# A decode layer on one core: the query projection in rows of 512, wo's last rows as 2 KB rows reordered on TensorE, W_down's last rows loaded at the end of the queue

## Chip, cores, metric

One core of a Trainium2 chip. The metric is the device time of one execution in microseconds, the median of repeated runs. The profile's span (first to last recorded instruction) is about 1.26 us shorter than the time.

## The reference

```python
# x [2,1,512]; k_cache, v_cache [2,32,8192,128]; wq [512,4096]; wo [4096,512]
# W_gate, W_up [512,1376]; W_down [1376,512]; all bf16
h  = x + A(layernorm(x))          # A: q = x@wq; softmax(q.K/sqrt(128)) @ V per head; then @ wo
h2 = h + B(layernorm(h))          # B: (relu(x@W_gate) * (x@W_up)) @ W_down
```

Two batch rows, 32 heads, 8192 cached keys: 268 MB of K and V are read once, and each is used with a single query. The weights are 12.6 MB more.

## The kernel before

One tile is K or V of two heads of one batch row: 128 partitions of 32 KB, 4 MB. Four slots hold two K and two V tiles. SyncE issues all large loads, in order, on one queue spread over 16 DMA engines.

The start of the queue, and the query projection (cut):

```python
nc.sync.dma_start(slot[3][:], A_wq...).then_inc(sem_wq, 16)
load(0, A_k_cache, 0)
load(1, A_v_cache, 0)
nc.sync.dma_start(wo_last[:].rearrange("p (h n) -> p h n", n=D),          # 256 runs of 1 KB
    A_wo[128 * DR:].rearrange("(h d) n -> d h n", d=128)).then_inc(sem_wl, 16)
nc.sync.dma_start(wd_last[:], B_W_down[F - FR:]).then_inc(sem_wd[3], 16)  # 96 runs of 1 KB
load(2, A_k_cache, 1)
# ... layernorm of x, transposed ...
for h in range(H):
    for c in range(DC):                                                   # 128 matmuls, 2 columns each
        i = nc.tensor.matmul(Wp[:, h*B:(h+1)*B], lhsT=wq[:, c, h*Dh:(h+1)*Dh], rhs=lT[:, c*B:(c+1)*B], ...)
# ... qT -> q_all: eight rounds of a DVE copy, four matmuls, one ScalarE copy ...
```

The loop over pairs of tiles (cut). VectorE multiplies 96 of the 128 key columns of a K tile with q and adds; TensorE does the other 32 through transposes, then all of P·V. The K slot is refilled after VectorE's multiply and TensorE's last transpose:

```python
run_d(k_mult(q)); last_d(); nc.vector.sem_inc(d2s, 1)     # VectorE has read the K tile
...
sp.wait((d2s, p + 1), tokp("kf", p)); load(s, A_k_cache, p + 2)
```

The end of the kernel (cut): W_up, W_gate and W_down go into the slot of the last-but-one K tile. W_up and W_gate become 44 small matmuls each; W_down is 11 blocks f of 4 matmuls, in the order of four DMAs:

```python
pe.wait((sem_wd[3], 16), t_hd)
order = [(10, 3)] + [(f, k) for k, (r0, n) in enumerate(WD_BLOCKS) for f in range(r0, r0 + n)]
for n, (f, k) in enumerate(order):
    pe.wait((sem_wd[k], 16))
    for m in range(4):
        i = nc.tensor.matmul(Op[0][32*m:32*m+B, 0:128], lhsT=hd[0:kp, f*B:(f+1)*B], rhs=..., ...)
```

A block in the text below is 256 instructions of a program unless it is called a block of W_down.

The softmax here doesn't subtract the row's maximum and nothing guards it: scores larger than these inputs give would overflow.

## Time and profile before

| | before |
|---|---|
| time, median of 3 | 661.2 us (661.18 to 661.27) |
| bytes moved, mean rate | 281.17 MB, 426 GB/s |
| spacing of 4 MB tiles, landing to landing, 50 to 625 us | 9.71 us |
| VectorE's first multiply in the loop | 26.05 us |
| last landing / last W_down matmul starts / end of span | 656.36 / 657.02 / 659.7 us |

The profile page of the kernel before. In the rows of forty slices a DMA digit of 9 is a share of 90% or more. The line that begins with q8 is the queue that brings instructions: packets, MB, share of the 16 engines' time. The last line is the summary of the chain that ended last.

```profile
span 659.7 us, 7791 instructions
...
DMA  9999999999999999999999999999999999999997
...
DMA packets 10781, 281.17 MB, mean 426 GB/s; under 512 B 1202, under 2 KB 1556, under 8 KB 1940
...
q8 instruction: 5, 0.08, 0.0%
...
DMA 80%; DVE 18%; issue 1%; PE 1%; SPq 0%; DVEq 0%
```

The queue is never empty: this is a kernel bound by its bytes. The 18% of VectorE in the chain are the multiplies that free a K slot; each is followed in the chain by a load of 32 us, of which only 9.7 us are its own transfer, the rest is queueing behind earlier tiles. So a quicker VectorE would only lengthen that queueing.

The timeline of the kernel before at the start of its loop (start, duration, engine, line, operation; in brackets the idle time before it and what ended it):

```profile
24.43 1.09 ACT L300 ACTIVATE q_all<-O 128x512 bf16<-128x512 f32 x2 [0.28 <-PE O L295]
26.05 6.56 DVE L514 TENSOR_TENSOR prod<-slot,q_c 128x12288 bf16<-128x12288 bf16 x1 [2.02 <-POOL q_c L511]
32.70 0.33 SPq L169 DMA_DIRECT2D slot<-in_A_k_cache_dram  x1
```

The load that this first multiply sets free is issued at 32.70 us and lands at 73.39 us, for X, V1 and the rest of K1 are ahead of it. Some 30 us of it are slack.

The chain of waits of the kernel before, its last pieces in order of time (start, length, what):

```profile
627.07 26.18 DMA slot<-in_B_W_gate_dram
...
653.30 1.73 PE O L730 x44
...
655.13 0.18 DVE hd L763
...
655.46 1.01 PE O L782 x29
656.47 0.28 issue
656.74 0.61 PE O L782 x14
```

W_gate lands, 44 matmuls, the gated product hd, and W_down's 44 matmuls, among which there is a hole. The timeline of the same matmuls:

```profile
655.46 0.28 PE L782 MATMUL O<-wd_last,hd 96*2 96x128 bf16 x4 [0.31 <-DVE ve L773]
655.52 0.95 PE L782 MATMUL O<-slot,hd 128*2 128x128 bf16 x25
656.74 0.59 PE L782 MATMUL O<-slot,hd 128*2 128x128 bf16 x15 [0.28 <-issue]
```

Matmul starts are exact in the records, ends are modelled. From the start of the 29th matmul (656.16) to that of the 30th (656.74) TensorE starts nothing for 0.59 us. The releaser is "issue", that is, none that the profile shows, and the 30th carries no wait; the wait for the last W_down DMA stands six weight loads later.

### The profile page before, as it was taken

How to read it: one execution, taken by the hardware profiler on the slowest of the kernel's cores; microseconds unless marked ns; L12 is line 12 of the kernel's file. 1: busy time of each engine (PE TensorE's matmuls, PEld its weight loads, DVE VectorE, ACT ScalarE, POOL GpSimd, SP SyncE). 2: the span in 40 equal slices, each digit the busy share in tenths (PEclk: the TensorE clock that was granted, in tenths of full speed). 3: DMA queues.
4: the chain of work that ended last, by engine and by line, in shares of the span. 5: the costliest groups of instructions: out<-in, count | busy, mean ns of one | idle time of the engine just before them, and what ended most of it. 6: DMA issues, size and time to landing. Idle time of an engine off the chain costs nothing.

```text
span 659.7 us, 7791 instructions
## 1 busy us (share of the span) xinstructions
PE 323.9 (49%) x3173; PEld 194.0 (29%) x3173; DVE 471.7 (71%) x285; ACT 211.9 (32%) x428; POOL 72.1 (11%) x121
## 2 busy tenths in 40 slices
PE   2653344435456443635545363554446554353577
PEld 2431322223233222323323242322324322132344
DVE  1775576788767678776768867676876767787991
ACT  0622332243342233333223243323324322333240
POOL 2002002020200202020020201102020110202000
PEclk9999995567755567675555757555575555657657
DMA  9999999999999999999999999999999999999997
GB/s 382 431 416 427 439 421 443 429 429 437 421 442 423 439 431 427 437 423 439 431 431 435 423 441 421 441 435 423 437 424 437 431 431 435 425 439 423 439 417 291
DMA packets 10781, 281.17 MB, mean 426 GB/s; under 512 B 1202, under 2 KB 1556, under 8 KB 1940
## 3 DMA queue, kind: packets, MB, share of 16 engines
q1 hardware_dynamic: 10760, 281.06, 99.3%
q8 instruction: 5, 0.08, 0.0%
q14 instruction: 4, 0.03, 0.0%
q10 hardware_dynamic: 12, 0.00, 0.0%
HBM read 281.05 MB, written 0.00 MB: 426 GB/s over the span
## 4 chain that ended last, share of the span: by engine, by line
DMA 80%; DVE 18%; issue 1%; PE 1%; SPq 0%; DVEq 0%
DMA slot<-in_A_k_cache_dram 76%; DVE prod L514 16%; DMA slot<-in_B_W_gate_dram 4%; DVE prod L523 2%; PE O L730 0%; PE O L782 0%; DVE scores L528 0%; SPq L169 0%; SPq L175 0%; DVEq L561 0%; SPq L178 0%; DVEq L565 0%; SPq L172 0%; DVE kT L789 0%; DVE hd L763 0%
## 5 line engine op out<-in xcount | busy, mean ns | idle before, releaser
L514 DVE TENSOR_TENSOR prod<-slot,q_c 128x12288 bf16<-128x12288 bf16 x32 | 209.9, 6558 | 145.8 <-DMA slot<-in_A_k_cache_dram 142.7
L379 PE MATMUL O<-slot,e 128*16 128x512 bf16 x1024 | 118.4, 617 | 220.0 <-ACT e L469 146.3
L523 DVE TENSOR_TENSOR prod<-prod 128x6144 bf16<-128x6144 bf16 (+3 forms) x128 | 212.3, 1658 | 7.8
L540 ACT ACTIVATE kT<-T 128x1024 bf16<-128x1024 bf16 x128 | 126.2, 1022 | 145.9 <-PE T L355 143.3
L355 PE MATMUL T<-ident_f,slot 128*128 128x128 f32 x512 | 111.5, 373 | 29.1 <-DVEq L561 29.0
L379 PEld LDWEIGHTS O<-slot,e 128*16 128x16 bf16 x1024 | 26.3, 113 | 286.3 <-ACT e L469 173.0
L469 ACT ACTIVATE e<-scores 64x96 bf16<-64x96 f32 x64 | 19.4, 304 | 239.7 <-DVEq L575 238.9
L355 PEld LDWEIGHTS T<-ident_f,slot 128*128 128x128 f32 x512 | 80.9, 191 | 44.3 <-DVEq L561 44.3
L511 POOL COPY q_c<-q_all 128x136 bf16<-128x136 bf16 x32 | 57.2, 1789 | 197.8 <-DVEq L565 167.8
L338 PE MATMUL S<-q_c,kT 128*128 128x4 bf16 x1024 | 47.5, 168 | 39.6 <-ACT kT L540 38.9
L338 PEld LDWEIGHTS S<-q_c,kT 128*128 128x128 bf16 x1024 | 39.4, 104 | 67.1 <-ACT kT L540 65.9
L391 PE MATMUL Ob<-sel,os_sb 128*128 128x4 f32 x136 | 30.1, 345 | 24.0 <-ACT os_sb L543 24.0
L391 PEld LDWEIGHTS Ob<-sel,os_sb 128*128 128x128 f32 x136 | 28.7, 312 | 25.9 <-ACT os_sb L543 25.9
L494 POOL MEMSET O_l<- 128x40 bf16 (+1 forms) x13 | 1.8, 136 | 303.8 <-DVEq L572 303.8
L528 DVE TENSOR_REDUCE scores<-prod 128x96 f32<-128x768 bf16 x32 | 30.5, 953 | 2.8
L540 ACT ACT_TABLE_LOAD x15 | 19.2, 1283 | 0.3
L469 ACT ACTIVATE e<-S 64x32 bf16<-64x32 f32 x64 | 13.0, 202 | 15.1 <-PE S L338 14.7
L543 ACT ACTIVATE os_sb<-O 128x512 f32<-128x512 f32 x17 | 10.2, 597 | 11.8 <-PE O L379 11.4
L469 ACT ACTIVATION_READ_ACCUMULATOR e<-S 64x1 f32 x64 | 12.8, 201 | 0.7
L469 ACT ACTIVATION_READ_ACCUMULATOR e<-scores 64x1 f32 x64 | 11.8, 184 | 0.0
L400 PEld LDWEIGHTS Ob<-zs,ones_f 128*128 128x128 f32 x30 | 7.3, 305 | 12.8 <-issue 12.8
L300 ACT ACTIVATE q_all<-O 128x512 bf16<-128x512 f32 x8 | 4.3, 595 | 17.7 <-PE O L295 17.7
(94 smaller groups left out, 91.7 us busy)
## 6 DMA issues: line engine op xcount, KB each, us to landing
slot<-in_A_k_cache_dram SPq DMA_DIRECT2D x32, 4096.0 KB, 32.1
slot<-in_A_v_cache_dram SPq DMA_DIRECT2D x31, 4096.0 KB, 30.3
slot<-in_A_wq_dram SPq DMA_DIRECT2D x1, 4096.0 KB, 12.2
X<-in_A_wo_dram SPq DMA_DIRECT2D x1, 3840.0 KB, 46.6
slot<-in_A_v_cache_dram SPq DMA_DIRECT2D x1, 3072.0 KB, 23.1
slot<-in_B_W_up_dram SPq DMA_DIRECT2D x1, 1376.0 KB, 23.2
slot<-in_B_W_gate_dram SPq DMA_DIRECT2D x1, 1376.0 KB, 26.2
slot<-in_A_v_cache_dram SPq DMA_DIRECT2D x1, 1024.0 KB, 25.2
```

The source lines that it names most:

```text
L338: i = nc.tensor.matmul(Sp[p % 2][:, 2 * jj:2 * jj + 4], lhsT=kv_[:, k, r, :], rhs=q_c[p % 2][:, 4 * r:4 * r + 4], start=(r == 0), stop=(r ...
L355: i = nc.tensor.transpose(Tp[g % 2][:, k * 128:(k + 1) * 128], k_t[:, j:j + 2, :].rearrange("p j d -> p (j d)").bitcast(F32), ident_f[:])
L379: i = nc.tensor.matmul(Op[0][c:c + 16, :], lhsT=e_t[q][:, j // VJ, :], rhs=v_t[:, j:j + VJ, :].rearrange("p j d -> p (j d)"), start=(q == ...
L391: i = nc.tensor.matmul(Ob[:, 0:4], lhsT=os_sb[:, jj * Dh:(jj + 1) * Dh], rhs=sel[:, 4 * jj:4 * jj + 4], start=(jj == 0), stop=(jj == VJ - 1))
L400: return nc.tensor.matmul(bank[:, ZC:ZC + 8], lhsT=ones_f[:], rhs=zs[:], start=True, stop=True)
L469: i = nc.scalar.activation(out=e_t[q][h, j0 // VJ:j1 // VJ, 8 * q:8 * q + 8].rearrange("p g (j a) -> p g j a", a=2)[:, :, :, a], in_=src(h ...
L511: nc.gpsimd.tensor_copy(out=q_c[p % 2][:], in_=q_all[:, p]).then_inc(g2d, 1)
L514: return nc.vector.tensor_tensor(out=prod[:, 0:JC, :], in0=tile((2 * p) % 4)[:, 0:JC, :], in1=q_c[p % 2][:, 8:QW].unsqueeze(1).broadcast_t ...
L523: run(nc.vector.tensor_tensor(out=prod[:, 0:JC, 0:w], in0=prod[:, 0:JC, 0:w], in1=prod[:, 0:JC, w:2 * w], op=ALU.add))
L528: return nc.vector.tensor_reduce(out=scores[p % PG][:, 0:JC], in_=prod[:, 0:JC, 0:8], axis=AX.X, op=ALU.add)
L540: to_pe(nc.scalar.activation(out=kT[gg % 2][:], in_=Tp[gg % 2][:].bitcast(BF16), func=ACT.Copy))
L543: to_pe(nc.scalar.activation(out=os_sb[:], in_=Op[0][:], func=ACT.Copy))
```

## The change

The intent: fewer, wider matmuls in the projection, fewer small packets, and a start of the queue without the 352 rows of 1 KB.

```diff
                 nc.sync.dma_start(slot[3][:], A_wq.rearrange("(p c) n -> p (c n)", c=DC)).then_inc(sem_wq, 16)
+                nc.sync.dma_start(
+                    wo_rows, A_wo[128 * DR:].rearrange("(p r) n -> p (r n)", r=2)).then_inc(sem_wl, 16)
                 load(0, A_k_cache, 0)
                 load(1, A_v_cache, 0)
-                nc.sync.dma_start(
-                    wo_last[:].rearrange("p (h n) -> p h n", n=D),
-                    A_wo[128 * DR:].rearrange("(h d) n -> d h n", d=128)).then_inc(sem_wl, 16)
-                nc.sync.dma_start(wd_last[:], B_W_down[F - FR:]).then_inc(sem_wd[3], 16)
                 load(2, A_k_cache, 1)
 # ... cut: the constants pick and place, made on GpSimd ...
-                for h in range(H):
+                for i in range(2):
                     for c in range(DC):
-                        i = nc.tensor.matmul(
-                            Wp[:, h * B:(h + 1) * B], lhsT=wq[:, c, h * Dh:(h + 1) * Dh],
-                            rhs=lT[:, c * B:(c + 1) * B], start=(c == 0), stop=(c == DC - 1))
+                        for t in range(4):
+                            n = (2 * t + i) * 512
+                            mm = nc.tensor.matmul(
+                                Op[i][32 * t:32 * t + B, :], lhsT=lT[:, c * B:(c + 1) * B], rhs=wq[:, c, n:n + 512],
+                                start=(c == 0), stop=(c == DC - 1))
 # ... cut: two evictions, 8 transposes; then in place of eight DVE copies and 32 matmuls:
+                for m in range(8):
+                    for a in range(2):
+                        mm = nc.tensor.matmul(
+                            Op[m % 2][64 * a:64 * a + 64, :], lhsT=pick[:, m, :],
+                            rhs=q_row.rearrange("p (m a d) -> p m a d", a=2, d=Dh)[:, :, a, :], start=True, stop=True)
 # ... one ScalarE copy each, as before ...
+                pe.wait((sem_wl, 16))
+                for h in range(2):
+                    for r in range(2):
+                        mm = nc.tensor.matmul(
+                            Tp[h][:], lhsT=place[:, h, r, :], rhs=wo_rows[:, r * D:(r + 1) * D], start=(r == 0), stop=(r == 1))
+                    t = pe.run(mm)
+                    act.wait(t)
+                    t_wl = act.run(nc.scalar.activation(out=wo_last[:, h * D:(h + 1) * D], in_=Tp[h][:], func=ACT.Copy))
 # ... at the end of the queue, behind the other W_down blocks:
+                        nc.sync.dma_start(wd_last[:], B_W_down[F - FR:]).then_inc(sem_wd[3], 16)
-                pe.wait((sem_wd[3], 16), t_hd)
-                order = [(10, 3)] + [(f, k) for k, (r0, n) in enumerate(WD_BLOCKS) for f in range(r0, r0 + n)]
+                pe.wait(t_hd)
+                order = [(f, k) for k, (r0, n) in enumerate(WD_BLOCKS) for f in range(r0, r0 + n)] + [(10, 3)]
```

## The prediction

> **What bounds the kernel now.** The profile page counts 281.17 MB moved at a mean 426 GB/s, and the row of DMA shares is 9 in every slice but the last. The chain of waits that ended last is 80% DMA and 18% the DVE multiply that frees a K slot. That DVE share is no bottleneck: the queue is never empty. From landing to landing of the 4 MB tiles the trace shows 9.71 us all the way from 50 to 625 us. So time is bytes, plus the start, plus what follows the last landings (the timeline: W_gate 653.3, last W_down block 656.4, last W_down matmul 657.3, output copies 657.8, end 659.7).
>
> **The three parts, costed.**
>
> 1. Query projection. Before: 128 matmuls with 2 columns (3.6 us), then eight DVE copies, 32 matmuls and eight ScalarE copies; the loop's first multiply starts at 26.05 us. After: 32 matmuls of 512 columns, two evictions, 8 transposes, 16 matmuls, the same eight ScalarE copies of about 0.6 us, two more for wo. I estimate a loop start 1 to 3 us earlier. Worth nothing: the K slot freed by that multiply (32.7 us) is refilled by a load behind 10 MB in the queue, landing at 73.4 us; there is some 30 us of slack.
>
> 2. wo rows. Its 256 packets of 1 KB took 46 ns each, W_down's 128 packets of 2 KB took 85 ns: over 16 engines 0.74 against 0.68 us. The median landings show wo_last costing 0.82 us. Gain about 0.1 us, directly on the DMA stream. The Trainium skill, "DMA: Bandwidth & Descriptors", section "Why small descriptors are slow", names a fixed overhead per packet; the packet times agree.
>
> 3. wd_last (96 KB, 0.38 us by landing times) moves from the early queue to its end. Same bytes; up, gate and the other W_down blocks land about 0.5 us earlier, the last landing about 0.2 us earlier, and 4 matmuls instead of 8 follow it.
>
> 4. A side effect. 100 fewer matmuls: some 200 PE instructions less before the loop. The Trainium skill, "Runtime: NRT & Kernel Launch", section "Instruction fetch mechanics", says blocks of 256 instructions are fetched by DMA. This trace shows five 16 KB instruction packets, the last at 654.15 us, and a PE pause inside the last W_down matmuls, 656.16 to 656.74, at which no semaphore wait stands: I read it as a block arriving late. After, I count one fetch fewer, and the last boundary falls near the start of the W_down matmuls, where its block should be there in time. Each fetch also leaves one DMA engine about 1.4 us late for good (a tile's sixteen landing marks: one straggler after the first, two after the second), and the slowest engine sets every landing. They fell on different engines, so one fewer should not change the maximum (1.8 us).
>
> **Sum.** 0.1 to 0.2 us from the stream, 0.3 to 0.6 us from the end of W_down: about 0.7 us. I predict 660.5 us, range 659.7 to 661.3. Faster by over 2%: 1%; within 2%: 98%; slower by over 2%: 1%.
>
> **What would show it right.** Four instruction packets of 16 KB; tile spacing still 9.71 us; the loop starting earlier without K2 landing earlier than by 0.2 us; no pause inside the last W_down matmuls; last matmul near 656.6 us; tail from last matmul to end still 2.3 us.
>
> **What would make it wrong.** Two fetches on one DMA engine would make it about 3 us late and cost about 1.4 us. A pause at the moved block boundary would return the gain. If the small rows at the queue's end land with more delay than amid large ones, W_down ends no earlier.

## The result

The changed kernel takes 660.47 us (median of 6 runs, 660.21 to 660.55); the kernel before beside it 661.21 us (6 runs, 660.97 to 661.27). The ratio is 0.9989, with a 95% interval of 0.9976 to 1.0001. Ratios are the mean time of one kernel's runs over that of the other's of the same rounds, so not quite the ratio of the medians. The interval lies far inside 2% and contains 1, so by itself it does not show which kernel is faster. In this measurement and in two controls on two different chips (below) the medians differ by -0.74, -0.60 and -0.78 us, and in the first and the last of them every run of the changed kernel was below every run of the one before.

The page of the changed kernel:

```profile
span 659.2 us, 7582 instructions
...
DMA packets 10653, 281.17 MB, mean 427 GB/s; under 512 B 1202, under 2 KB 1300, under 8 KB 1812
...
q8 instruction: 5, 0.08, 0.1%
...
DMA 76%; DVE 19%; PE 4%; issue 1%; ACT 1%; SPq 0%; DVEq 0%
```

128 packets fewer (256 of 1 KB became 128 of 2 KB), the same bytes, and 209 executed instructions fewer. Tiles still land 9.71 to 9.72 us apart. The 4% of PE in the chain are new; where they come from is seen below. The timeline at the start of the loop:

```profile
23.67 1.08 ACT L318 ACTIVATE q_all<-O 128x512 bf16<-128x512 f32 x2 [0.25 <-PE O L312]
25.12 0.60 ACT L329 ACTIVATE wo_last<-T 128x512 bf16<-128x512 f32 x1 [0.36 <-PE T L325]
25.93 0.60 ACT L329 ACTIVATE wo_last<-T 128x512 bf16<-128x512 f32 x1 [0.21 <-PE T L325]
26.85 6.56 DVE L540 TENSOR_TENSOR prod<-slot,q_c 128x12288 bf16<-128x12288 bf16 x1 [5.73 <-ACT wo_last L329]
```

The loop starts 0.8 us later, not earlier: ScalarE's eight copies take their 0.6 us each as before, the two copies of wo come behind them, and VectorE waits for those. The chain at the end of the changed kernel:

```profile
651.30 1.71 PE S L756 x44
653.01 0.34 PE T L767 x14
653.36 1.66 PE O L756 x44
...
655.13 0.19 DVE hd L789
...
655.36 1.37 PE O L808 x23
```

W_gate is no longer in this chain: it landed at 652.5 us and TensorE came to it at 653.3. And the W_down matmuls of its timeline:

```profile
655.36 1.23 PE L808 MATMUL O<-slot,hd 128*2 128x128 bf16 x40 [0.22 <-DVE hd L789]
656.38 0.32 PE L808 MATMUL O<-wd_last,hd 96*2 96x128 bf16 x4
```

All 44 run in one go; the last starts at 656.39 us instead of 657.02. That is 0.63 us sooner; the spans differ by 0.55 us, for what follows that matmul took 0.08 us longer. The sum: hd starts at the same 655.13 us in both; the first W_down matmul follows 0.10 us sooner (0.23 instead of 0.33 us behind hd); the hole of 0.59 us is gone; the 44 matmuls themselves took 0.05 us more. (The profiled pair is one execution of each kernel; below, other executions lose their time elsewhere.)

### The profile page after: what moved, and what is told of

It reads as the page before. It is cut to its first block, busy times and chain, and to the rows that moved or that the text cites. A ratio compares the mean times of both kernels' runs of the same rounds, so it can differ in the third digit from the quotient of the medians.

```text
span 659.2 us, 7582 instructions
## 1 busy us (share of the span) xinstructions
PE 324.3 (49%) x3073; PEld 188.6 (29%) x3073; DVE 469.2 (71%) x280; ACT 213.6 (32%) x431; POOL 73.5 (11%) x125
## 4 chain that ended last, share of the span: by engine, by line
DMA 76%; DVE 19%; PE 4%; issue 1%; ACT 1%; SPq 0%; DVEq 0%
DMA slot<-in_A_k_cache_dram 76%; DVE prod L540 16%; DVE prod L549 2%; PE O L405 1%; PE O L463 1%; PE T L381 0%; ACT kT L566 0%; PE W L469 0%; DVE scores L554 0%; PE S L756 0%; PE O L756 0%; PE O L808 0%; PE Ob L417 0%; SPq L172 0%; PE S L364 0%
## 5 line engine op out<-in xcount | busy, mean ns | idle before, releaser
L381 PE MATMUL T<-ident_f,slot 128*128 128x128 f32 x512 | 108.6, 365 | 29.1 <-DVEq L587 29.1
L381 PEld LDWEIGHTS T<-ident_f,slot 128*128 128x128 f32 x512 | 79.0, 188 | 44.2 <-DVEq L587 43.3
L525 POOL COPY rsel<-rows 128x30 bf16<-128x30 bf16 x28 | 5.9, 209 | 33.3 <-DVEq L598 32.5
```

The costliest lines, as they stand in the source:

```text
L381: i = nc.tensor.transpose(Tp[g % 2][:, k * 128:(k + 1) * 128], k_t[:, j:j + 2, :].rearrange("p j d -> p (j d)").bitcast(F32), ident_f[:])
```

## The experiments

The question is which part brings this, and why. The theory of the prediction: the hole is TensorE waiting for a block of instructions that its DMA has not yet brought, because the queue is full of weights; 206 instructions fewer before the loop move that block's boundary. The rival: what counts is the landing of the last weights, so the part that loads at the end brings most, and the parts add up.

All twelve runs gave correct results. Each was timed in 5 rounds, four kernels to a chip. Medians in us:

| kernel | time | before, same chip | span (median of its runs) | span before, same chip |
|---|---|---|---|---|
| wd_alone | 660.83 | 661.04 | 659.6 | 659.8 |
| q_alone | 660.67 | 661.04 | 659.4 | 659.8 |
| wo_alone | 661.05 | 661.04 | 659.8 | 659.8 |
| after_pad | 660.62 | 661.04 | 659.4 | 659.8 |
| after_same | 660.52 | 661.12 | 659.3 | 659.9 |
| before_pad | 661.84 | 661.12 | 659.7 | 659.9 |
| late_loop | 660.31 | 661.12 | 659.1 | 659.9 |
| hr_late | 660.40 | 661.12 | 659.2 | 659.9 |
| after_ctl | 660.42 | 661.20 | 659.2 | 660.0 |
| not_wd | 661.13 | 661.20 | 659.8 | 660.0 |
| not_wo | 660.30 | 661.20 | 659.1 | 660.0 |
| hr_late_b | 660.32 | 661.20 | 659.1 | 660.0 |

The intervals of the ratios are all about 0.13% to each side (0.9 us), so a single difference of 0.2 us in this table is not resolved. What decides are the traces: in each the last W_down matmul can be followed back to what it waited for.

| profiled run | hd starts | first W_down matmul | hole (us) | last landing | last W_down matmul | what was last |
|---|---|---|---|---|---|---|
| before | 655.13 | 655.46 | 0.59 | 656.36 | 657.02 | hole, behind the chain to hd |
| after | 655.13 | 655.36 | none | 656.06 | 656.39 | TensorE's chain to hd |
| wd_alone | 655.15 | 655.39 | 0.47 | 656.09 | 656.85 | hole, behind the chain to hd |
| q_alone | 655.29 | 655.62 | none | 656.53 | 656.65 | landing |
| wo_alone | 655.66 | 655.99 | 0.18 | 656.39 | 657.04 | chain to hd, hole |
| after_pad | 655.41 | 655.65 | 0.07 | 656.40 | 656.68 | chain to hd, hole |
| after_same | 655.24 | 655.48 | none | 656.08 | 656.51 | chain to hd |
| before_pad | 655.35 | 655.67 | 0.26 | 656.58 | 656.87 | chain to hd, hole |
| late_loop | 655.26 | 655.49 | none | 656.04 | 656.52 | chain to hd |
| hr_late | 654.46 | 654.69 | none | 656.03 | 656.08 | landing |
| after_ctl | 654.52 | 654.76 | none | 656.12 | 656.18 | landing |
| not_wd | 655.69 | 656.02 | 0.15 | 656.35 | 657.11 | chain to hd, hole |
| not_wo | 654.50 | 654.73 | none | 656.30 | 656.35 | landing |
| hr_late_b | 654.79 | 655.02 | none | 656.36 | 656.41 | landing |

The holes are read from the records of single weight loads and matmuls, at a place where no wait stands. In wo_alone and after_pad the number is the gap between two weight loads; some matmuls still start in it, and the stretch in which TensorE starts nothing at all is 0.07 us in each. The last landing is the last of the sixteen marks with which a DMA's sixteen parts report.

### The parts alone: wd_alone, q_alone, wo_alone

wd_alone is the kernel before with this edit:

```diff
-                nc.sync.dma_start(wd_last[:], B_W_down[F - FR:]).then_inc(sem_wd[3], 16)   # early
+                        nc.sync.dma_start(wd_last[:], B_W_down[F - FR:]).then_inc(sem_wd[3], 16)   # last in the queue
-                order = [(10, 3)] + [...]
+                order = [...] + [(10, 3)]
```

> The kernel before with one part of the change: the last rows of W_down load at the end of the queue and are multiplied last. The PE program keeps its length. Theory (a late instruction block): the pause of about 0.6 us inside the last W_down matmuls stays, because the block is fetched when it was before; last matmul starts at about 657.0 us of the profile, time 0 to 0.15 us below before. Rival (the landing of the last weights is what counts, the parts add up): the last landings come earlier with only 4 matmuls after them, so 0.4 to 0.6 us below before.

Measured: 0.21 us below before by medians, between the two expectations and nearer to the theory; W_gate lands 0.7 us earlier, the last landing 0.27 us earlier, and yet hd starts when it did, and the hole is still there. Its timeline:

```profile
655.39 1.01 PE L782 MATMUL O<-slot,hd 128*2 128x128 bf16 x29 [0.22 <-DVE ve L773]
656.57 0.48 PE L782 MATMUL O<-slot,hd 128*2 128x128 bf16 x11 [0.16 <-issue]
```

Though other matmuls stand here now (wd_last is no longer the first), the hole is behind the 29th, as before. A wait for the data of one W_down DMA would have moved with that data; a place in the program does not.

q_alone is the changed kernel with wo and W_down loaded as in the kernel before:

```diff
-                nc.sync.dma_start(wo_rows, ...)        # and place, its 4 matmuls, its 2 copies
+                nc.sync.dma_start(wo_last[:].rearrange("p (h n) -> p h n", n=D), ...)   # behind V0, as before
+                nc.sync.dma_start(wd_last[:], B_W_down[F - FR:]).then_inc(sem_wd[3], 16)
-                order = [...] + [(10, 3)]
+                order = [(10, 3)] + [...]
```

> The kernel before with the query projection of the change alone (rows of 512); wo and W_down load as before. The PE program is about 210 instructions shorter. Theory (late block): no pause in the last W_down matmuls; the last W_down block lands near 656.4 us with 8 matmuls after it, last matmul starts near 656.75, time 0.2 to 0.35 us below before. Rival (landing alone): same as before within 0.1 us.

Measured: 0.37 us below before by medians. No hole; the last eight matmuls wait 0.14 us for the landing at 656.53; the last matmul starts at 656.65. The trace is as the theory has it. The loop starts at 24.48 us, 1.6 us earlier than before.

wo_alone is the kernel before with wo's rows as 2 KB packets:

```diff
+                nc.sync.dma_start(wo_rows, A_wo[128 * DR:].rearrange("(p r) n -> p (r n)", r=2))...
                 load(0, A_k_cache, 0)
                 load(1, A_v_cache, 0)
-                nc.sync.dma_start(wo_last[:].rearrange("p (h n) -> p h n", n=D), ...)
+                # ... place, 4 matmuls and 2 ScalarE copies before the loop, as in the change
```

> The kernel before with wo's last rows as 2 KB packets right behind wq, reordered on TensorE. 8 PE instructions more. Both theories: the queue gains about 0.1 us; theory (late block): the pause hides most of it, 0 to 0.15 us below before; rival (landing alone): 0.1 us below before.

Measured: the same as before (+0.01 us). W_gate's median landing comes 0.27 us earlier than before (651.63 against 651.90), more than the 0.1 us predicted for the queue, and none of it reaches the end: TensorE's chain was later in this run, see below.

### Putting the block boundary back, and moving it alone: after_pad, before_pad

```diff
+                for _ in range(103):      # after_pad; 25 in before_pad, which is the kernel before
+                    nc.tensor.matmul(Ob[:, 0:8], lhsT=onesn[:], rhs=ident[:, 0:8], start=True, stop=True)
                 nc.tensor.matmul(Ob[:, 0:ZC + 8], lhsT=onesn[:], rhs=ident[:, 0:ZC + 8], start=True, stop=True)
```

> The changed kernel with 103 small matmuls before the loop, so that its PE program has exactly the length of the kernel before (206 instructions more) and the block boundary falls where it fell before. They delay the loop start by some 3 us, which the slack should swallow. Theory (late block): the pause comes back, last matmul near 657.0, time 0.4 to 0.7 us above the changed kernel, so near that of before. Rival (landing alone): no change against the changed kernel, about 0.75 us below before.

> The kernel before with 25 small matmuls before the loop and nothing else: 50 PE instructions more, which move the last block boundary from inside the last W_down matmuls to their start, where the block has had longer to arrive. Refined theory: the pause is gone; then the last W_down block's landing near 656.4 rules, last matmul near 656.7, time 0.2 to 0.4 us below before, although the kernel only does more work. Rival (the block's arrival does not matter, the pause was something else): pause and time as before.

As a size both expectations failed. after_pad: 660.62 us, 0.1 to 0.2 us above the three medians of the changed kernel; the hole came back at its place but was only 0.07 us long. before_pad: the time is 0.7 us above before, not below, though its span is 0.2 us shorter. Its timeline:

```profile
655.67 0.28 PE L784 MATMUL O<-wd_last,hd 96*2 96x128 bf16 x4 [0.31 <-DVE ve L775]
655.95 1.24 PE L784 MATMUL O<-slot,hd 128*2 128x128 bf16 x40
```

The hole is not gone but has moved, to behind the fourth matmul, and is 0.26 us long.

As to the place of the hole the two settle the matter, together with wd_alone, wo_alone and not_wd (below). Each matmul is a weight load and a multiplication, two instructions. Counting weight loads of W_down from 0, the first one behind the hole is:

| kernel | PE instructions against before | first weight load behind the hole | expected from the count | it starts at | hole (us) |
|---|---|---|---|---|---|
| before | 0 | 30 | | 656.74 | 0.59 |
| wd_alone | 0 | 30 | 30 | 656.57 | 0.47 |
| after_pad | 0 | 30 | 30 | 656.32 | 0.07 |
| wo_alone | +8 | 26 | 26 | 656.66 | 0.18 |
| before_pad | +50 | 5 | 5 | 655.95 | 0.26 |
| not_wd | -206, that is +50 less 256 | 5 | 5 | 656.18 | 0.15 |
| after | -206, that is +50 less 256 | none | 5 | | none |

In six programs the hole sits at the instruction that the count of instructions names, whatever data stands there. It is a block boundary. The timeline of not_wd (the 40 matmuls behind the first four start 0.15 us late, their weight loads do not):

```profile
656.02 0.28 PE L808 MATMUL O<-wd_last,hd 96*2 96x128 bf16 x4 [0.31 <-DVE ve L799]
656.03 1.09 PEld L808 LDWEIGHTS O<-slot,hd 128*2 128x2 bf16 x40
656.18 1.24 PE L808 MATMUL O<-slot,hd 128*2 128x128 bf16 x40
```

That the hole is TensorE waiting for the block to arrive is an inference from the 16 KB instruction packets, and it fits four of the six. In before, wd_alone, wo_alone and after_pad the last packet ahead of the hole starts at 654.15, 654.01, 654.14 and 653.86 us, and the hole ends 2.5 to 2.6 us later each time. There the hole's length is a race between TensorE and the block: in after_pad hd was 0.28 us later and the hole's end 0.42 us sooner than in the kernel before, so little of it was left. My expectation had taken its length for fixed. In before_pad and not_wd the packet starts as early as 652.30 and 652.67 us and the hole ends 3.6 and 3.5 us later, while the changed kernel, with its packet at 652.38 us, passes the same place at 655.4 us without a hole. Why these two have one is not shown; besides the old order of the W_down matmuls they share the late packet told next.

What before_pad shows besides: its time less its span is 1.9 to 2.2 us in four of its five runs, against 1.26 us elsewhere. A sixth 16 KB instruction packet starts at 661.02 us in its trace, after the last instruction at 659.7 us. not_wd shows the same (a packet at 661.08, 2.3 us and more in two of its runs), and single runs of the kernel before too (up to 2.3 us). What sets off this late packet is not settled by these runs; that before_pad's runs are longer outside the span and not inside it is shown.

### The start of the loop: late_loop

```diff
                 dve.wait(t_q_b, t_wl, t_const)
                 dve.last()
+                dve.run(nc.vector.memset(prod[:], 0.0))
+                for _ in range(2):
+                    dve.last()
+                    dve.run(nc.vector.tensor_tensor(
+                        out=prod[:, :, 0:64], in0=prod[:, :, 0:64], in1=prod[:, :, 64:128], op=ALU.add))
+                dve.last()
```

> The changed kernel with three VectorE operations over the product buffer ahead of its loop, so that the loop starts some 10 to 20 us later; PE's program is untouched. If the start of the loop has the slack that I read (about 30 us): within 0.2 us of the changed kernel. Rival (the projection's length is part of the time): slower by as much as the loop starts later.

The timeline of late_loop:

```profile
28.18 5.18 DVE L573 MEMSET prod<- 128x6144 uint32 x1 [6.71 <-issue]
33.40 6.75 DVE L576 TENSOR_TENSOR prod<-prod 128x6144 bf16<-128x6144 bf16 x2
40.42 6.56 DVE L540 TENSOR_TENSOR prod<-slot,q_c 128x12288 bf16<-128x12288 bf16 x1 [0.27 <-DVE prod L576]
```

The loop starts 13.4 us later than in after_same (40.42 against 27.05), and the time is 660.31 us against its 660.52, all within the scatter. The start of the loop has slack, as read; the shape of the projection's matmuls is worth nothing by its own duration. What the projection gives, it gives by its number of instructions, as far as these runs show.

### One part taken out: not_wd, not_wo

not_wd undoes the W_down part of the changed kernel, not_wo the wo part:

```diff
 # not_wd
+                nc.sync.dma_start(wd_last[:], B_W_down[F - FR:]).then_inc(sem_wd[3], 16)   # early, behind V0
-                        nc.sync.dma_start(wd_last[:], B_W_down[F - FR:]).then_inc(sem_wd[3], 16)
-                pe.wait(t_hd)
-                order = [...] + [(10, 3)]
+                pe.wait((sem_wd[3], 16), t_hd)
+                order = [(10, 3)] + [...]
 # not_wo
-                nc.sync.dma_start(wo_rows, ...)       # and place, 4 matmuls, 2 copies
+                nc.sync.dma_start(wo_last[:].rearrange("p (h n) -> p h n", n=D), ...)   # 1 KB packets, behind V0
```

> The changed kernel without its last part: W_down's last rows load early again and are multiplied first. Refined theory (latest of TensorE chain, block, landing): last block of W_down lands at 656.0 to 656.3 us with 8 matmuls behind it, no pause, last matmul at 656.4 to 656.7, time 0 to 0.25 us above the changed kernel. Rival (the parts add up, and loading at the end is most of the gain): 0.4 us or more above it.

> The changed kernel with wo's last rows loaded as 1 KB packets behind V0 again, not reordered on TensorE. Refined theory: the loop starts near 24.5 us instead of 26.9 (two evictions less), which is worth nothing; landings at the end come 0.1 to 0.3 us later; time 0 to 0.25 us above the changed kernel. Rival (the loop's start counts): faster than the changed kernel by some 2 us.

not_wo: as expected of the theory, if anything a little faster than the changed kernel (660.30 against 660.42 us); its loop starts at 24.55 us, its last landing 0.18 us later. The wo part gives nothing to the time. not_wd missed my expectation: 0.7 us above the changed kernel by time and 0.6 us by span. Part is the late packet after the span in two of its runs. In its trace the first W_down matmul comes 0.33 us behind hd, against 0.24 in after_ctl, and the hole of 0.15 us follows. The largest part is that hd starts 1.2 us later than in after_ctl: W_gate lands 0.6 us later (653.22 against 652.63), with wd_last ahead of it in the queue again, and TensorE's chain comes to it later still (653.86). That chain needs a word.

### TensorE's own chain in the tail: after_same, after_ctl, hr_late

From about 629 us on TensorE is busy almost without a break until hd. Busy times of the five engines in one stretch, for the kernel before and the changed kernel (stretch, length, busy time and instructions of PE, PEld, DVE, ACT, POOL; then granted clock, DMA share, GB/s):

```profile
642.00:648.00 6.00, 5.65 (x66) 1.97 (x66) 1.50 (x4) 1.85 (x9) 0.00 (x0) 0.72 0.97 405
```

```profile
642.00:648.00 6.00, 5.99 (x62) 1.88 (x53) 0.67 (x3) 0.75 (x4) 0.00 (x0) 0.59 1.00 418
```

The granted clock in the tail goes up and down: in these fourteen traces the full clock comes in stretches of 3.4 or 6.8 us behind 600 us, and which stretch has it differs from run to run of the same kernel. In the profiled pair the changed kernel had its tiles 0.7 us earlier and lost it to a lower clock (0.59 against 0.72 in this stretch), so that hd started at the same time. In after_ctl, the same kernel on another chip, hd starts at 654.52, and there the last landing rules. In four traces (wd_alone, wo_alone, after_pad, not_wd) the records show no full clock at all between 605 and 645 us; those four start the 30 matmuls of wo at 630.1 to 630.8 us, the other ten, which have one, at 628.8 to 629.7. So about 1 us of this chain goes with where the full clock falls. Less of it reaches hd, which W_gate's landing also holds back: hd starts at 655.15 to 655.69 us in those four and at 654.46 to 655.35 in the others. These runs do not show what sets the clock, so not_wd's miss, and the exact shares of the single parts, remain open.

hr_late shortens that chain by moving 16 matmuls to where TensorE waits for VectorE anyway:

```diff
                 t_u = ffn_in(Sp[1], wup, 0, FC)
-                for k in range(4): ...          # 16 matmuls: h over the partitions
-                t_hr = pe.run(i)
                 pe.wait((sem_w[1], 16))
                 t_g = ffn_in(Op[1], wgt, 0, FC)
                 # ... the 8 matmuls of the variance ...
+                for k in range(4): ...
+                t_hr = pe.run(i)
```

> Control: the changed kernel once more, on the chip of the following three runs. Refined theory (the last W_down matmul starts at the latest of three times: the tail's own chain on TensorE plus W_down's 1.0 us; the arrival of the last instruction block; the last landing): no pause, last matmul 656.3 to 656.7 us, time 0.5 to 0.9 us below before. Rival (the gain on the first chip was the state of that chip): within 0.2 us of before.

> The changed kernel with the 16 matmuls that spread h over the partitions moved from between W_up and W_gate to behind W_gate, where PE waits for the gated product; no instruction more or less. Refined theory: in the changed kernel the tail's chain on TensorE is what ends last, so the gated product comes 0.3 us earlier and the end 0.1 to 0.25 us earlier, until the last landing rules (656.1). Rival (landings rule the end of the changed kernel): no change.

> Control: the changed kernel a third time, beside the next three on the same chip. Both theories: 0.5 to 0.8 us below before, no pause, last W_down matmul at 656.3 to 656.6 us, last landing near 656.1.

> The variant with the spreading of h moved behind W_gate, once more beside the changed kernel. Refined theory: its W_down matmuls wait for landings at three blocks, the last one starts at about the last landing (656.0 to 656.1), span 0.1 to 0.35 us and time 0.05 to 0.3 us below the changed kernel. Rival (landings already ruled before): equal within 0.05 us in the profile's last matmul.

The controls repeat the result (0.60 and 0.78 us below before). In hr_late's trace the DMA is back in the chain at its end:

```profile
626.42 26.14 DMA slot<-in_B_W_gate_dram
...
652.61 1.72 PE O L756 x44
```

W_down's matmuls now wait for three landings in turn and the last starts 0.05 us behind the last landing, in both runs of this variant. The times are 0.12 and 0.10 us below the changed kernel of the same chip, in the expected direction, but the runs of the two overlap; as a gain this is not resolved. Nor do the two traces show that the edit moved the limit: after_ctl, without it, also starts its last matmul 0.06 us behind the last landing, with hd at 654.52. As a version it beats both kernels by its medians and costs nothing.

## Why the prediction was right, and where its steps were not

- **The total** (660.5 predicted, 660.47 measured) and its source, the end of W_down, hold. That the size fits so closely is partly luck: in the profiled pair the hole (0.59 us) and 0.10 us that I had not seen make it up, while the 0.1 to 0.2 us of the stream and the earlier landings of up and gate brought nothing. The last W_down matmul was predicted near 656.6 and started at 656.39; the tail behind it (from that matmul's modelled end) was predicted 2.3 us and is 2.5 in the changed kernel, 2.4 before.
- **The hole** sits at a boundary of instruction blocks. This was an inference from one trace; the table of six programs shows it. That it is a block arriving late fits the packets of four of them and is open in two. That its removal alone gives 0.3 to 0.6 us does not hold: the hole's length varies (0.07 to 0.59 us).
- **The loop start**, "an estimate of 1 to 3 us earlier", was wrong for the changed kernel: 0.8 us later in its first profile (26.85), 26.15 to 27.05 in the controls. What the projection saved (1.6 us in q_alone) the two wo copies took back, since VectorE waits for them. The conclusion that it is worth nothing is shown by late_loop.
- **wo's packets**: 0.1 us was too small for the queue (0.27 us in W_gate's median landing), and too large for the time: wo_alone is level with before, and not_wo loses nothing that these runs resolve.
- **wd_last**: up and gate "about 0.5 us earlier" were 0.74 us earlier in their last landing (wo's 0.27 us is in that), the last landing 0.30 us instead of 0.2. The step that failed is what they bring: I took hd to follow W_gate's landing. In the changed kernel TensorE's chain, at half clock most of the time, ends later than that landing; in the profiled pair all 0.7 us were lost there. It also brought 0.1 us that I had not seen. In the old order a separate wait for hd stands ahead of the first weight load (at 655.35 us in the kernel before); in the new one the weight load itself waits for hd, and the separate wait is for W_down's first DMA, which had landed. The first matmul follows hd by 0.33 us in the five traces with the old order and by 0.23 to 0.24 us in the nine with the new.
- **My own sign for slack was wrong**: "without K2 landing earlier than by 0.2 us". K2's last landing came 0.77 us earlier (72.62 against 73.39), and wd_last and part of wo's cost were no longer ahead of it, as my own points 2 and 3 say.
- **Four instruction packets** were predicted; there are five. One more packet starts at 655.95 us, 0.6 us behind the first W_down matmul; no hole in the span goes with it.
- **Stragglers** stayed as predicted: after each of the first two 16 KB instruction packets one more of a tile's sixteen marks comes late, and the spread of the last DMA's marks was 1.82 us before and 1.93 us after.
- **Which part?** By the medians both the shorter PE program and the late wd_last are needed for the whole gain: alone they give 0.37 and 0.21 us, and without wd_last 0.07. Differences of this size are inside the intervals, so the shares are not shown. The limits at the end (TensorE's chain, the instruction block, the last landing) lie within half a microsecond of one another, so removing one mostly shows the next.

## What to carry to other kernels

When a kernel is bound by one stream from start to end, count only what happens behind the last landings, and list everything that ends there; several limits can lie within a few tenths of a microsecond, and a change to one of them shows only down to the next. A hole in an engine at which no wait stands can be an instruction block that comes late: check whether it stays at the same instruction count when the data around it moves, before you explain it by data. When two kernels differ by 0.1%, one timing says little; read in several traces what the last instruction waited for.

## What the Trainium skill lacked or had wrong

- "Runtime: NRT & Kernel Launch", section "Instruction fetch mechanics": it calls the cost of a block boundary "one DMA tail-bump, mostly hidden". Here it was not always hidden: holes of 0.07 to 0.59 us in TensorE at the boundary in six programs, none in the other eight traces. It is in agreement on the block (16 KB packets).
- The same page does not say that a fetch costs the data queue too: after each of the first two 16 KB instruction packets one more of the sixteen parts of every later DMA was about 1.4 us late. In the kernel before the marks of a tile spread over 0.44 us before the first packet, with one straggler at 1.87 us after it and two (1.73 and 1.87 us) after the second.
- No page has the packet that starts after the last instruction (661.02 us in before_pad), nor that time less span then grows from 1.26 us to about 2.1 (before_pad) or 2.3 us and more (not_wd).
- "TensorE: Matmul & The Clock Gate", section "What's actually happening": sustained activity is said to release the throttle after at least one busy window of about 3.4 us; it does not say how busy. In the kernel before, TensorE was busy in 2.72, 3.15 and 2.65 us of the three such windows from 631.71 to 641.95 us, and no full clock followed; it was busy throughout from 641.95 to 645.36 us, and the full clock followed. But in the changed kernel it was busy throughout from 633.29 to 636.70 us too, and the next 10 us stayed at 0.50. (Busy time is the profile's, with modelled ends.) The length of the stretches at full clock, 3.4 or 6.8 us, agrees.
- "DMA: Bandwidth & Descriptors", section "Why small descriptors are slow", agrees in kind with the packet times (1 KB 46 ns, 2 KB 85 ns), but does not have what the large packets behind the small rows paid: most of the first 32 KB packets behind the 1 KB rows took about 1.43 us, against a mean of 1.22 us.
